# Splitting the second layer's output weights during part 1, and loading values, keys and half of the raw weights in the second half of each batch

## Chip, cores and metric

One of a Trainium2 chip's cores runs the kernel. The metric is device microseconds from start to end of one execution; less is better. Besides the times there is one execution under the hardware profiler, with a trace of every instruction and DMA packet.

## What is computed

Attention through 32 packed queries per head, then two feed-forward blocks on the result, all in fp32:

```python
def sm_attn(qq, kk, vv):                  # scale = 1/sqrt(64)
    a = softmax(scale * qq @ kk.T); return a @ vv
p_packed = sm_attn(p, k, v)               # p: 8 x 8 x 32 x 64;  q, k, v: 8 x 8 x 576 x 64
x = sm_attn(q, p_packed, p_packed)        # then as 4608 tokens x 512
x = maximum(maximum(x @ w1, x @ w2), x @ w3) @ w_out     # 512 -> 768 -> 512
g = softplus(x @ w_in2)                                  # 512 -> 2048
return g @ w_out2                                        # 2048 -> 512
```

The weights arrive as 64-bit numbers and are turned into fp32 in the kernel ("narrowing").

## The kernel before

**Numbers as pairs.** A matmul on TensorE that should keep fp32's precision is done with operands split into a high part `hi` in the format fp32r and the rest `lo`, as three matmuls: hi by hi, hi by lo, lo by hi. A split is two instructions (L125 to L128): ScalarE copies the source into `hi`, then VectorE (or GpSimd) computes `lo = src - hi`.

**Part 1** goes through the eight batches (attention and the first block). In each batch of the loop at L827 (n = 1 to 6) TensorE does the first block of batch n (18 units `U`, 12 matmuls each; four blocks `L`, 36 each) with the attention of batch n + 1 in between. Everything is put into instruction order by hand: the string `batch` (L815) lists names, each appearance advances that step up to its next `yield`, and every engine, SP's queue of DMA issues among them, keeps that order strictly. The names that matter here: `Lq0..3`, `Lk0..3`, `Lv`, `Lp` load raw queries, keys, values and packed queries; `Tq`, `Tk` transpose them; `S` and `A` are the score matmuls, `V` the values, `AX` the second softmax; `LS` splits a maxout result; `D` issues the stores of finished tokens. Beside this the loop prepares the weights of part 2: `R` (L770) issues a load of one 512 KB block of raw 64-bit weights, `N` (L762) narrows the oldest loaded block once `AHEAD` of them have been issued (GpSimd `low_bits`, ScalarE `rebase`, VectorE `combine`), `W` (L697) issues the stores of what is ready, and `Q` (L758) is an empty step. There are 32 blocks: 16 of the input weights `wi2`, then 16 of the output weights `wo2` (L689). Two blocks of `wo2` give, with four subtractions on GpSimd (L748 to L754), the left sides of seven products: both layers of part 2 use Strassen's scheme, so seven products P1 to P7 stand for eight. For the output weights these seven fp32 matrices of 128 x 256 per pair are stored to DRAM as `wof`.

The last batch (L853) has no attention to do and prepares part 2 instead: `loadx`, `sumx`, `splitx` for tokens, `load`, `sum`, `split` for weights.

**Part 2** (from L985) runs the second block in five chunks of tokens, c = 0 to 4: three of 2 x 512 and two of 2 x 384. In a chunk layer 3 has eight steps j (`layer3`, L1050, 42 matmuls each at L1047) and layer 4 has 28 slots v (`layer4`, L1121, 12 matmuls each at L1140), 336 matmuls in each layer. A slot multiplies a split activation tile, `ghi` and `glo` (`split_g`, L1106, three slots ahead, three buffers each), with a weight tile `wc` of seven products. The tiles wc, 1792 KB each, stand in a ring of three. From chunk 1 on they are read back already split, from `wic` (layer 3) and `woc` (layer 4) in DRAM (`get_weights`, L1027). In chunk 0 they are made first: layer 3's from `wi32` by sums and a split, layer 4's by loading seven units of `wof` (`load_units`, L998) and splitting them (`split_weights`, L1012, two halves of 128 x 1024 and 128 x 768), and each is stored by `put_weights` (L1021). For layer 4 this is done at fixed slots (L1229 to L1237):

```python
for t in range(6):
    v = 7 * t // 2 + 1
    for part in range(2):
        jobs[v + part].append((split_weights, FP + t + 2, part))
    if t >= 1 and FP + t + 3 < STEP:
        jobs[v + 1].append((load_weights, FP + t + 3))
    ...
    jobs[v + 2].append((put_weights, FP + t + 2))
```

and for the first two of the eight tiles in steps j = 6, 7 of layer 3 (L1206). Layer 4's VectorE also forms sums and differences of activations (`form`, L1104), sums and splits the next chunk's tokens (`sum_x2`, `split_x2`, at slots 6, 11, 15, 20 and 7, 12, 16, 21 in chunk 0) and moves results out of PSUM (`result`, slots 13, 19, 23, 27).

The functions that the diff touches, and what calls them:

Of the kernel before, what the change touches and what calls it, by code (L numbers as in the profile page):

```python
# [19 lines left out]
def packed_attention_maxout_softplus(  # L20
# [22 lines left out]
    nc = tc.nc  # L43
# [34 lines left out]
    wof = dram.tile([len(PRODUCTS), FP, P, 2 * P], F32, name="wof")  # L78
    woc = dram.tile([FP, P, 2 * 7 * 2 * P], F32, name="woc")
# [58 lines left out]
    nwp = a_ctx.enter_context(tc.tile_pool(name="nwp", bufs=3))  # L138
# [8 lines left out]
    tp = at_ctx.enter_context(tc.tile_pool(name="tp", bufs=2, side="right"))  # L147
    stp = at_ctx.enter_context(tc.tile_pool(name="stp", bufs=5, side="right"))
# [540 lines left out]
    to_narrow = [  # L689
# [4 lines left out]
    ] + [(wo2[f * P : f * P + P, :], (f % FP, f // FP)) for j in range(FP) for f in (j, j + FP)]  # L694
# [6 lines left out]

    def units(j, *names):
        at = [PRODUCTS.index(name) for name in names]
        if len(at) == 1:
            return wof[at[0], j]
        step = at[1] - at[0]
        return wof[at[0] : at[1] + 1 : step, j].rearrange("i p x -> p i x")
# [9 lines left out]
    def narrow_wo_steps(raw64, j, k):  # L717
# [23 lines left out]
        if k == 0:  # L741
            upper[j] = b
            to_store.append((units(j, "P1"), b[:, 0]))
            return
        to_store.append((units(j, "P2", "P3"), b))
# [9 lines left out]
        to_store.append((units(j, "P6", "P5"), t[:, 0:2]))  # L755
        to_store.append((units(j, "P7", "P4"), t[:, 2:4]))

    def split_next():  # L758
        return
        yield  # L760

# [15 lines left out]
    AHEAD = 2  # L777

    def in_batch(n, name):
# [10 lines left out]
        if a == "PW":  # L790
            return packed_weight_steps(n if i else m, i)
        return {
            "Lv": lambda: once(load_v, m),
# [22 lines left out]
            U0 W0 Lq0 D3 N0 PW1 U0 Lq1 N0 U1 PW1 PW1 PP U2 U1 PP W1 N1 Lq2 U3 U2 LS0 LS0 U4  # L816
            U3 N1 W2 R0 N2 PW2 U4 S PW2 Lq3 Lp N2 SX0 U5 Lv SX1 SX0 PW2 W3 SX1 U6 U5 R1 LS1
            VS0 VS1 U7 LS1 U6 Lk0 Tq0 N3 U8 U7 Tq1 Lk1 PW3 U8 LS2 E0 N3 PW3 LS2 E1 R2 U9 E0
            PW3 W4 E1 U10 Lk2 U9 Tq2 N4 U11 U10 Tq3 U12 U11 Lk3 LS3 PW4 R3 N4 LS3 U12 W5 V
            PW4 PW4 U13 VS0 VS1 N5 U14 U13 R4 U15 U14 N5 LS4 LS4 PT U15 U16 PT U17 U16 A U17  # L820
            LS5 PW0 AX0 LS5 AX1 L0 PW0 AX0 R5 AX1 AX0 AX1 AX0 PW0 AX1 AX0 L1 L0 AX1 AX0 AX1
            D0 AX0 AX1 AX0 AX1 X0 L2 L1 X0 X1 X1 D1 Tk0 Tk1 Tk2 L3 L2 Tk3 D2 L3
    """
    with tc.manual_schedule(engines={E.PE, E.DVE, E.Activation, E.Pool, E.SP}):
        for g in range(NH):
            transpose_kq(2, g, "k")
        for n in range(1, B - 1):  # L827
# [170 lines left out]
    def load_units(t):  # L998
        u = wus[FP + t] = up.tile([P, 8, 2, P], F32, tag="u", name="wu")
        flat = wof.rearrange("i j p x -> (i j) p x")  # L1000
        nc.sync.dma_start(
            out=u[:, 1:8].rearrange("p m b x -> p m (b x)"),
            in_=flat[7 * t : 7 * t + 7].rearrange("m p x -> p m x"),
        )

    def load_weights(s):
        if s < FP:
            load_pair(s)
        elif s < STEP:
            load_units(s - FP)  # L1010

# [9 lines left out]
    def put_weights(s):  # L1021
        nc.sync.dma_start(
            out=(wic[s] if s < FP else woc[s - FP]),
            in_=pairs[s].rearrange("p h a k x -> p (h a k x)").bitcast(F32),
        )

    def get_weights(s):  # L1027
        if STEP <= s < STEP * NCH:
            r = s % STEP
            nc.sync.dma_start(  # L1030
                out=pair_tile(s).rearrange("p h a k x -> p (h a k x)").bitcast(F32),
                in_=(wic[r] if r < FP else woc[r - FP]),
            )
# [87 lines left out]
    def layer4(c, v):  # L1121
# [8 lines left out]
        for i in range(2):  # L1130
            u = 2 * (v % NU) + i
            tile_no, at = divmod(pos * FP + u, 7)
            w = pairs[STEP * c + FP + tile_no]
# [180 lines left out]
```

## Time and profile before

| | |
|---|---|
| three runs, us | 1224.98, 1220.55, 1224.32 (median 1224.32) |
| the profiled execution | 1225.36 us, of which the span of its instructions is 1223.6 us |
| mean granted TensorE clock | 0.993 of full speed |
| busy in the span | TensorE matmuls 98%, weight loads 86% (beside them), VectorE 68%, ScalarE 43%, GpSimd 17% |
| moved by DMA | 272.26 MB, on average 223 GB/s |

The page of the profile gives one execution. "Busy" is the time in which an engine's instructions run; idle time is put down to what ended it last. In the trace PE is TensorE's matmul side, PEld its weight loads, DVE VectorE, ACT ScalarE, POOL GpSimd, and SPq the queue of DMA issues on SP. A line such as L128 can be a helper's, so groups are told apart by the names of the tiles: `glo<-a,ghi` and `wc<-wu,wc` are both splits of L128.

### The profile page before, as it was taken

How to read it: one execution, taken by the hardware profiler on the slowest of the kernel's cores; microseconds unless marked ns; L12 is line 12 of the kernel's file. 1: busy time of each engine (PE TensorE's matmuls, PEld its weight loads, DVE VectorE, ACT ScalarE, POOL GpSimd, SP SyncE). 2: the span in 40 equal slices, each digit the busy share in tenths (PEclk: the TensorE clock that was granted, in tenths of full speed). 3: DMA queues.
4: the chain of work that ended last, by engine and by line, in shares of the span. 5: the costliest groups of instructions: out<-in, count | busy, mean ns of one | idle time of the engine just before them, and what ended most of it. 6: DMA issues, size and time to landing. Idle time of an engine off the chain costs nothing.

```text
span 1223.6 us, 21279 instructions
## 1 busy us (share of the span) xinstructions
PE 1196.2 (98%) x8599; PEld 1055.3 (86%) x8599; DVE 829.1 (68%) x1182; ACT 528.4 (43%) x782; POOL 211.0 (17%) x224
## 2 busy tenths in 40 slices
PE   8899999999999999999979999999999999999998
PEld 6688989898989899888757888888888899999998
DVE  2976656575666648678999456894568745874585
ACT  4744443435253434545555234552345423542343
POOL 1422212123242502241000031000310012000100
PEclk9999999999999999999989999999999999999999
DMA  9898686859696721667677955469554597678665
GB/s 244 262 251 196 175 217 179 220 168 255 184 245 190 226 70 36 240 252 269 226 241 282 327 195 191 181 211 331 188 193 181 197 364 267 241 236 320 250 255 144
DMA packets 117283, 272.26 MB, mean 223 GB/s; under 512 B 14784, under 2 KB 90304, under 8 KB 106944
## 3 DMA queue, kind: packets, MB, share of 16 engines
q1 hardware_dynamic: 114976, 269.13, 69.1%
q10 hardware_dynamic: 2208, 1.77, 0.5%
q8 instruction: 67, 1.10, 0.4%
q14 instruction: 32, 0.26, 0.1%
HBM read 211.09 MB, written 59.77 MB: 221 GB/s over the span
## 4 chain that ended last, share of the span: by engine, by line
PE 87%; DVE 7%; DMA 3%; issue 1%; ACT 1%; SPq 0%; DVEq 0%; ACTq 0%
PE ps L482 31%; PE ps L1047 27%; PE ps L1140 22%; PE ps_w L460 3%; DVE glo L128 2%; PE ps_s L287 2%; DVE x2lo L128 1%; DMA wc<-wic 1%; DVE wc L128 1%; DMA qraw<-in_q_dram 1%; PE ps_v L358 1%; PE ps_e L331 1%; DVE a L1104 1%; DMA wu<-wof 1%; DMA praw<-in_p_dram 0%
## 5 line engine op out<-in xcount | busy, mean ns | idle before, releaser
L1047 PE MATMUL ps<-x2hi,wc 128*128 128x512 f32 (+1 forms) x1120 | 322.1, 367 | 2.5 <-DMA wc<-wic 1.1
L1140 PE MATMUL ps<-ghi,wc 128*128 128x512 f32 (+1 forms) x1120 | 323.8, 369 | 0.4 <-ACT ghi L126 0.4
L1061 DVE TENSOR_TENSOR h<-h,ps 128x512 f32<-128x512 f32 (+1 forms) x280 | 173.0, 632 | 156.9 <-PE ps L1047 110.6
L1047 PEld LDWEIGHTS ps<-x2hi,wc 128*128 128x128 f32 x1120 | 207.2, 188 | 29.8 <-DVE h L1061 1.4
L1140 PEld LDWEIGHTS ps<-ghi,wc 128*128 128x128 f32 x1120 | 208.3, 189 | 27.1 <-ACT ghi L126 0.8
L1140 PE MATMUL ps<-glo,wc 128*128 128x512 f32 (+1 forms) x560 | 209.1, 373 | 8.9 <-DVE glo L128 8.5
L1047 PE MATMUL ps<-x2lo,wc 128*128 128x512 f32 (+1 forms) x560 | 205.6, 367 | 0.0
L1082 ACT ACTIVATE a<-h 128x512 f32<-128x512 f32 (+1 forms) x160 | 89.3, 585 | 221.9 <-DVE h L1061 210.2
L126 ACT ACTIVATE ghi<-a 128x1024 fp32r<-128x1024 f32 (+1 forms) x120 | 115.4, 972 | 97.4 <-PE ps L1140 88.2
L128 DVE TENSOR_TENSOR glo<-a,ghi 128x1024 fp32r<-128x1024 f32 (+1 forms) x120 | 131.7, 1110 | 31.7 <-ACT ghi L126 31.5
L1104 POOL TENSOR_TENSOR a<-a,a 128x512 f32<-128x512 f32 (+1 forms) x32 | 36.9, 1155 | 553.3 <-ACT a L1082 553.3
L1140 PEld LDWEIGHTS ps<-glo,wc 128*128 128x128 f32 x560 | 105.8, 189 | 29.8 <-DVE glo L128 16.6
L482 PE MATMUL ps<-a2hi,pwhi 128*128 128x288 f32 x576 | 128.5, 305 | 0.1
L482 PE MATMUL ps<-a2hi,pwlo 128*128 128x288 f32 x576 | 123.2, 295 | 0.4 <-DVE pwlo L128 0.4
L482 PE MATMUL ps<-a2lo,pwhi 128*128 128x288 f32 x576 | 123.2, 296 | 0.0
L1047 PEld LDWEIGHTS ps<-x2lo,wc 128*128 128x128 f32 x560 | 105.1, 188 | 13.2
L511 DVE TENSOR_TENSOR m<-ps,m 128x576 f32<-128x576 f32 x96 | 72.5, 755 | 57.0 <-PE ps L482 55.2
L482 PEld LDWEIGHTS ps<-a2hi,pwhi 128*128 128x128 f32 x576 | 91.6, 189 | 16.8 <-ACT m L509 5.3
L482 PEld LDWEIGHTS ps<-a2hi,pwlo 128*128 128x128 f32 x576 | 92.6, 189 | 0.7 <-DVE pwlo L128 0.7
L482 PEld LDWEIGHTS ps<-a2lo,pwhi 128*128 128x128 f32 x576 | 92.8, 189 | 0.0
L128 POOL TENSOR_TENSOR hlo<-m,hhi 128x576 fp32r<-128x576 f32 x41 | 59.1, 1440 | 189.9 <-ACT hhi L126 165.2
L482 PE MATMUL ps<-hhi,wo_hi 128*128 128x288 f32 x384 | 83.1, 298 | 0.0
(107 smaller groups left out, 1470.1 us busy)
## 6 DMA issues: line engine op xcount, KB each, us to landing
wc<-wic SPq DMA_DIRECT2D x32, 1792.0 KB, 8.8
wc<-woc SPq DMA_DIRECT2D x32, 1792.0 KB, 7.4
qraw<-in_q_dram SPq DMA_DIRECT2D x112, 140.0 KB, 3.8
wic<-wc SPq DMA_DIRECT2D x8, 1792.0 KB
woc<-wc SPq DMA_DIRECT2D x8, 1792.0 KB, 11.3
kraw<-in_k_dram SPq DMA_DIRECT2D x96, 140.0 KB, 5.5
vt<-in_v_dram SPq DMA_DIRECT2D x8, 1152.0 KB, 11.0
wraw<-in_moe_w_dram SPq DMA_DIRECT2D x18, 512.0 KB, 7.5
```

What stands on the lines that cost most here:

```text
L126: nc.scalar.activation(out=hi, in_=src, func=AF.Copy)
L128: engine.tensor_tensor(out=lo, in0=src, in1=hi.bitcast(F32), op=ALU.subtract)
L287: nc.tensor.matmul(ps[G][cols, hh, :HS], w[rows, cols], x[rows, g, hh * HS : hh * HS + HS], start=True, stop=True,)
L331: nc.tensor.transpose(ps[: 32 * TI, i // hi, (i % hi) * P : (i % hi) * P + P], e[:, i], ident,)
L460: nc.tensor.matmul(ps[cols, G, : units * P].rearrange("p (w x) -> p w x", w=units), ppT[n][rows, cols], wsb[rows, 4 * c : 4 * c + units, g ...
L482: nc.tensor.matmul(o, w, xx, start=first, stop=last)
L511: nc.vector.tensor_tensor(out=m, in0=ps[:, :, :HS], in1=ms[n, f], op=ALU.max)
L1047: nc.tensor.matmul(out, l, r, start=(i == 0), stop=(i == len(terms) - 1))
L1061: add(out=h[:, o], in0=h[:, a], in1=ps, op=ALU.add)
L1082: nc.scalar.activation(out=g[half, k][:, j, :wide], in_=h[:, 2 * k + half], func=AF.Softplus)
L1104: engine.tensor_tensor(out=out, in0=in0, in1=in1, op=op)
L1140: nc.tensor.matmul(ps[b][:, :wide], l, r, start=first and u == 0 and head, stop=u == FP - 1 and tail, skip_group_check=not first,)
```

## The change

The seven products of the output weights are split where they are made, in part 1. Each pair of `wo2` blocks now queues four splits; the formerly empty step `Q` does one of them (ScalarE copies to `hi`, VectorE subtracts in place), and the next `W` stores both parts into `woc`, whose layout becomes one 2 KB row (hi, lo) per product, unit and partition. `wof`, its loads, the splits and the `put_weights` of layer 4 in chunk 0 go, and `get_weights` reads `woc` in chunk 0 as in the others, seven rows per partition instead of one of 14 KB. The order of the raw blocks is mixed (two of `wo2`, two of `wi2`, ...), `AHEAD` falls from 2 to 1, the tiles for narrowing get five buffers instead of three and move to the memory that is given up before the last batch. In the batch's order `Lv` loads the values one batch ahead behind `V`, the four `Lk` go behind `Tq3`, and three of the six `R` into the second half.

```diff
-    wof = dram.tile([len(PRODUCTS), FP, P, 2 * P], F32, name="wof")
-    woc = dram.tile([FP, P, 2 * 7 * 2 * P], F32, name="woc")
+    woc = dram.tile([len(PRODUCTS), FP, P, 2, 2 * P], F32, name="woc")
 
...
-    nwp = a_ctx.enter_context(tc.tile_pool(name="nwp", bufs=3))
+    nwp = at_ctx.enter_context(tc.tile_pool(name="nwp", bufs=5, side="right"))
...
-    to_narrow = [
+    wi_narrow = [
         (wi2[e * P : e * P + P, c * 1024 : c * 1024 + 1024],
          wi_blocks(c, e))
         for c in range(DF2 // 512)
         for e in range(KC)
-    ] + [(wo2[f * P : f * P + P, :], (f % FP, f // FP)) for j in range(FP) for f in (j, j + FP)]
+    ]
+    wo_narrow = [
+        (wo2[f * P : f * P + P, :], (f % FP, f // FP)) for j in range(FP) for f in (j, j + FP)
+    ]
+    to_narrow = []
+    for j in range(FP):
+        to_narrow += wo_narrow[2 * j : 2 * j + 2] + wi_narrow[2 * j : 2 * j + 2]
...
             upper[j] = b
-            to_store.append((units(j, "P1"), b[:, 0]))
             return
-        to_store.append((units(j, "P2", "P3"), b))
...
-        to_store.append((units(j, "P6", "P5"), t[:, 0:2]))
-        to_store.append((units(j, "P7", "P4"), t[:, 2:4]))
+        to_split.append((j, ("P1",), a[:, 0:1], a[:, 1:2]))
+        to_split.append((j, ("P6", "P5"), t[:, 0:2], None))
+        to_split.append((j, ("P2", "P3"), b, None))
+        to_split.append((j, ("P7", "P4"), t[:, 2:4], None))
 
     def split_next():
-        return
-        yield
+
+        if not to_split:
+            return
+        j, names, x, hi = to_split.pop(0)
+        at = [PRODUCTS.index(name) for name in names]
+        step = at[1] - at[0] if len(at) > 1 else 1
+        dst = woc[at[0] : at[-1] + 1 : step, j].rearrange("i p h x -> p i h x")
+        if hi is None:
+            hi = nwp.tile([P, 512], F32, tag="x32", name="hi32")
+            hi = hi.rearrange("p (i x) -> p i x", x=2 * P)
+        hi, lo = hi.bitcast(F32R), x.bitcast(F32R)
+        nc.scalar.activation(out=hi, in_=x, func=AF.Copy)
+        yield
+        nc.vector.tensor_tensor(out=lo, in0=x, in1=hi.bitcast(F32), op=ALU.subtract)
+        for h, half in enumerate((hi, lo)):
+            to_store.append((dst[:, :, h], half.bitcast(F32)))
...
-    AHEAD = 2
+    AHEAD = 1
...
-            "Lv": lambda: once(load_v, m),
+            "Lv": lambda: once(load_v, m + 1) if m + 1 < B else none,
...
     batch = """
-            U0 W0 Lq0 D3 N0 PW1 U0 Lq1 N0 U1 PW1 PW1 PP U2 U1 PP W1 N1 Lq2 U3 U2 LS0 LS0 U4
-            U3 N1 W2 R0 N2 PW2 U4 S PW2 Lq3 Lp N2 SX0 U5 Lv SX1 SX0 PW2 W3 SX1 U6 U5 R1 LS1
-            VS0 VS1 U7 LS1 U6 Lk0 Tq0 N3 U8 U7 Tq1 Lk1 PW3 U8 LS2 E0 N3 PW3 LS2 E1 R2 U9 E0
-            PW3 W4 E1 U10 Lk2 U9 Tq2 N4 U11 U10 Tq3 U12 U11 Lk3 LS3 PW4 R3 N4 LS3 U12 W5 V
-            PW4 PW4 U13 VS0 VS1 N5 U14 U13 R4 U15 U14 N5 LS4 LS4 PT U15 U16 PT U17 U16 A U17
-            LS5 PW0 AX0 LS5 AX1 L0 PW0 AX0 R5 AX1 AX0 AX1 AX0 PW0 AX1 AX0 L1 L0 AX1 AX0 AX1
-            D0 AX0 AX1 AX0 AX1 X0 L2 L1 X0 X1 X1 D1 Tk0 Tk1 Tk2 L3 L2 Tk3 D2 L3
+            U0 W6 Lp Lq0 Q0 N0 Q0 PW1 U0 N0 Lq1 U1 PW1 D3 PW1 R0 W0 PP U2 U1 PP Q1 N1 U3 U2
+            LS0 Lq2 Q1 LS0 U4 U3 N1 Q2 N2 PW2 U4 W1 Q2 S PW2 R1 N2 SX0 U5 Lq3 SX1 SX0 PW2 W2
+            SX1 U6 U5 LS1 VS0 VS1 U7 LS1 U6 Tq0 Q3 N3 U8 U7 Q4 Tq1 R2 PW3 U8 Q3 LS2 E0 N3
+            PW3 LS2 E1 Q4 U9 E0 PW3 E1 W3 U10 U9 Tq2 Q5 N4 U11 U10 Tq3 Q6 U12 U11 Lk0 LS3 Q5
+            PW4 N4 LS3 Q6 U12 V PW4 PW4 Q7 U13 VS0 W4 VS1 N5 Q8 U14 U13 Lk1 Q7 U15 U14 Lv N5
+            LS4 Q8 LS4 PT U15 U16 R3 PT W5 U17 U16 Lk2 A U17 LS5 PW0 AX0 R4 LS5 AX1 L0 PW0
+            AX0 AX1 AX0 Lk3 AX1 AX0 PW0 AX1 AX0 L1 L0 AX1 R5 AX0 AX1 AX0 AX1 D0 AX0 AX1 X0
+            L2 L1 X0 X1 X1 Tk0 Tk1 D1 Tk2 L3 L2 Tk3 D2 L3
     """
     with tc.manual_schedule(engines={E.PE, E.DVE, E.Activation, E.Pool, E.SP}):
         for g in range(NH):
             transpose_kq(2, g, "k")
+        load_v(2)
         for n in range(1, B - 1):
...
-    def load_units(t):
...
-    def load_weights(s):
...
     def put_weights(s):
         nc.sync.dma_start(
-            out=(wic[s] if s < FP else woc[s - FP]),
+            out=wic[s],
             in_=pairs[s].rearrange("p h a k x -> p (h a k x)").bitcast(F32),
         )
 
     def get_weights(s):
-        if STEP <= s < STEP * NCH:
-            r = s % STEP
-            nc.sync.dma_start(
-                out=pair_tile(s).rearrange("p h a k x -> p (h a k x)").bitcast(F32),
-                in_=(wic[r] if r < FP else woc[r - FP]),
-            )
+        r = s % STEP
+        if s >= STEP * NCH or s < FP:
+            return
+        flat = pair_tile(s).rearrange("p h a k x -> p (h a k x)").bitcast(F32)
+        if r < FP:
+            nc.sync.dma_start(out=flat, in_=wic[r])
+            return
+        rows = woc.rearrange("i j p h x -> (i j) p (h x)")[7 * (r - FP) : 7 * (r - FP) + 7]
+        nc.sync.dma_start(
+            out=flat.rearrange("p (m x) -> p m x", m=7), in_=rows.rearrange("m p x -> p m x")
+        )
...
-            w = pairs[STEP * c + FP + tile_no]
+            w = pairs[STEP * c + FP + tile_no].rearrange("p h a k x -> p (h a k x)")
+            w = w.rearrange("p (a h k x) -> p h a k x", a=7, h=2, k=2)
...
-                    for part in range(2):
-                        aside[1 + part].append((split_weights, j + 2, part))
-                    aside[3] += [(load_weights, j + 4), (put_weights, j + 2)]
+                        for part in range(2):
+                            aside[1 + part].append((split_weights, j + 2, part))
+                        if j + 4 < FP:
+                            aside[3].append((load_pair, j + 4))
+                        aside[3].append((put_weights, j + 2))
...
-                for t in range(6):
-                    v = 7 * t // 2 + 1
-                    for part in range(2):
-                        jobs[v + part].append((split_weights, FP + t + 2, part))
-                    if t >= 1 and FP + t + 3 < STEP:
-                        jobs[v + 1].append((load_weights, FP + t + 3))
-                    if t == 0:
-                        jobs[v + 1].append((load_x2, c + 1, 0))
-                    jobs[v + 2].append((put_weights, FP + t + 2))
+                jobs[2].append((load_x2, c + 1, 0))
```

## Rows read from the trace of the kernel before

**Rows 1.** Windows: length, PE, PEld, DVE, ACT, POOL busy (instructions), clock, DMA share, GB/s

```profile
337.00:395.70 58.70, 58.70 (x617) 53.07 (x616) 39.27 (x75) 24.05 (x39) 21.18 (x24) 1.00 0.79 222
...
507.70:584.00 76.30, 76.28 (x336) 63.17 (x337) 56.72 (x74) 37.95 (x56) 23.48 (x24) 1.00 0.73 265
584.00:676.20 92.20, 83.14 (x338) 63.88 (x337) 81.98 (x92) 48.60 (x55) 0.00 (x0) 0.96 0.70 242
676.20:752.60 76.40, 76.35 (x338) 62.86 (x336) 38.34 (x57) 24.09 (x39) 14.71 (x15) 1.00 0.71 250
752.60:829.00 76.40, 76.40 (x337) 62.95 (x336) 66.03 (x70) 38.74 (x43) 1.30 (x1) 1.00 0.56 191
...
981.80:1040.10 58.30, 58.30 (x338) 58.15 (x336) 30.74 (x57) 19.75 (x39) 12.76 (x15) 1.00 0.87 318
```

**Rows 2.** Waits of PE, whole span: us in total, times, longest us

```profile
PE ps L1140 <- DVE glo L128: 8.5, 8, 3.6
```

**Rows 3.** PE in order of time, chunk 0's layer 4: start, us, what, [idle before]

```profile
630.10 0.39 PE L1140 MATMUL ps<-glo,wc 128*128 128x512 f32 x1
...
635.16 0.80 PE L1140 MATMUL ps<-glo,wc 128*128 128x512 f32 x1 [3.55 <-DVE glo L128]
...
636.61 0.63 PE L1140 MATMUL ps<-glo,wc 128*128 128x512 f32 x1
```

**Rows 4.** Windows for tile wc alone, chunk 0's layer 4: columns without POOL

```profile
584.00:676.20 92.20, 83.14 (x338) 63.88 (x337) 13.00 (x12) 11.31 (x12) 0.96 0.70 242
```

**Rows 5.** Groups of DVE and ACT, chunk 0's layer 4: busy us, mean ns | idle

```profile
L885 DVE TENSOR_TENSOR xu<-xu 128x256 f32<-128x256 f32 x16 | 6.1, 420 | 0.1
...
L128 DVE TENSOR_TENSOR x2lo<-xu,x2hi 128x1024 fp32r<-128x1024 f32 x4 | 4.9, 1218 | 0.0
L1186 DVE STREAM_TRANSPOSE o<-mid 128x512 f32<-128x512 f32 x6 | 4.3, 712 | 0.2
L1184 DVE TENSOR_TENSOR mid<-mid,ps 128x512 f32<-128x512 f32 x6 | 4.0, 664 | 0.0
L128 DVE TENSOR_TENSOR x2lo<-xu,x2hi 128x768 fp32r<-128x768 f32 x4 | 3.8, 952 | 0.0
...
L126 ACT ACTIVATE ghi<-a 128x1024 fp32r<-128x1024 f32 x22 | 22.7, 1051 | 11.9 <-PE ps L1140 11.9
L126 ACT ACTIVATE wc<-wu 128x1024 fp32r<-128x1024 f32 x6 | 6.3, 1056 | 11.0 <-DMA wu<-wof 6.6 <-DMA xu<-x2d 4.4
```

**Rows 6.** Chain of waits, chunk 0's layer 4: start, us, what

```profile
602.87 1.14 DVE glo L128
```

**Rows 7.** Groups of DVE and ACT in the batch of rows 1, columns as there

```profile
L128 DVE TENSOR_TENSOR pwlo<-ps_w,pwhi 128x512 fp32r<-128x512 f32 x1 | 0.7, 691 | 0.6 <-ACT pwhi L126 0.6
...
L722 ACT ACTIVATE x<-raw 128x512 f32<-128x512 f32 x6 | 4.0, 674 | 9.2 <-DMA raw<-in_moe_w_out_dram 4.7 <-DMA kraw<-in_k_dram 4.5
```

**Rows 8.** Waits of all engines, batches 2 to 6 of the loop

```profile
ACT x L86 <- DMA raw<-in_moe_w_in_dram: 13.8, 4, 4.7
```

**Rows 9.** SP's queue, ACT and the chain on PE near the loop's start

```profile
98.41 5.14 SPq L553 DMA_DIRECT2D x2d<-xs  x2
...
110.16 0.65 ACT L509 ACTIVATE m<-ps 128x576 f32<-128x576 f32 x1
...
112.74 0.97 PE ps_s L287 x32
```

**Rows 10.** Tile raw: ns min/median/max of an operation, and its DMAs

```profile
L732 DVE SCALAR_TENSOR_TENSOR x<-x,raw x64: 276/284/1535, 285.2 to 422.3; 128x128 int32<-128x128 int32 x64
...
DMA to landing us min/median/max: 2.6/6.8/10.9
```

**Rows 11.** The page's DMA issues: KB each, median us to landing

```profile
wc<-woc SPq DMA_DIRECT2D x32, 1792.0 KB, 7.4
...
wu<-wof SPq DMA_DIRECT2D x8, 896.0 KB, 8.6
wof<-raw SPq DMA_DIRECT2D x16, 256.0 KB, 2.6
```

More of the change, by code (lines that the diff above doesn't have):

```diff
@@ L700, in store_narrowed @@
             nc.sync.dma_start(out=dst, in_=x)
[L702 to L707, printed above, removed]
     def narrow_wi_steps(raw64, dst):
@@ L996, in packed_attention_maxout_softplus @@
     STEP = 2 * FP
-    def load_units(t):
-        u = wus[FP + t] = up.tile([P, 8, 2, P], F32, tag="u", name="wu")
-        flat = wof.rearrange("i j p x -> (i j) p x")
-        nc.sync.dma_start(
-            out=u[:, 1:8].rearrange("p m b x -> p m (b x)"),
-            in_=flat[7 * t : 7 * t + 7].rearrange("m p x -> p m x"),
-        )
-    def load_weights(s):
[L1007 to L1010, printed above, removed]
     def split_weights(s, part):
@@ L1027, in get_weights @@
     def get_weights(s):
-        if STEP <= s < STEP * NCH:
-            r = s % STEP
-            nc.sync.dma_start(
-                out=pair_tile(s).rearrange("p h a k x -> p (h a k x)").bitcast(F32),
-                in_=(wic[r] if r < FP else woc[r - FP]),
-            )
+        r = s % STEP
[9 more added lines that the diff above has]
+        )
     def bank(name):
```

## Prediction, made before the changed kernel ran

> **What bounds the kernel now.** TensorE does, almost everywhere, so the first question is where it is not full. The windows cut at the stages answer it [rows 1]: a batch of part 1, chunk 0's two layers, chunk 1's two, and a layer of the narrower chunk 3. In a batch of part 1 PE is busy for the whole 58.70 us; the six batches of the loop all look so. In part 2 chunks 0 to 2 have the same 336 matmuls in every layer, and chunk 1 shows what they cost when nothing is late: 76.40 us in layer 3 and 76.40 in layer 4. Chunk 0's layer 3 takes the same, but its layer 4 takes 92.20 us, with PE busy for 83.14, VectorE for 81.98 and a granted clock of 0.96. That is 15.8 us over. The list of PE's waits names the cause [rows 2]: 8.5 us in 8 waits for `glo`, the low part of an activation split, the longest 3.6 us. In order of time that one stands at 635.16 [rows 3], after 3.55 us of idling, and behind it a matmul takes 0.63 us that took 0.39 before: with the granted clock at 0.96 over the stretch, TensorE ran for a few microseconds at 1.2 instead of 2.4 GHz. So the 15.8 are the recorded waits, the half clock behind the longest, and small gaps that the modelled ends cover.
>
> Why is `glo` late? In chunk 0 VectorE also splits weights: 12 instructions on `wc`, 13.00 us, with 11.31 us on ScalarE [rows 4], and ScalarE's copies of them sit idle for 11.0 us, 6.6 of it for the load of `wof` [rows 5]. Both engines work strictly in order, so a weight split whose data is not there holds the activation splits behind it. Chunk 1's VectorE does the same work without weights in 66.03 us and nobody waits [rows 1].
>
> **Removed from chunk 0.** Of layer 4: the 12 VectorE and 12 ScalarE instructions, four of the eight loads of `wof` and their waits, and six stores of `woc`. VectorE keeps 81.98 - 13.00 = 69.0 us in 76.4, three more than chunk 1, because 16 instead of 8 of the sums on `xu` stand here (6.1 us, so 3.0 for eight) [rows 5]. Since 69 of 76 is tight, I walk the worst stretch, slots 6 to 13. A slot is 76.4 / 28 = 2.73 us, eight are 21.8. VectorE has in them eight `glo` and six forms of the same size at 1.14 each from start to start [rows 6], two groups of four sums (4 x 0.42, overlapping, 1.5), two splits of tokens (1.22 + 0.95, overlapping, 2.0) and one result (2 x (0.71 + 0.66), 2.7) [rows 5]: 16.0 + 3.0 + 4.0 + 2.7 = 25.7. It falls 3.9 us behind. `glo` is made up to two slots ahead, 5.5 us, of which its own copy and subtraction take 1.05 + 1.14 [rows 5, 6], leaving 3.3. So it is about 0.6 us late around slot 14, and then recovers, since slots 14, 17 and 18 hold one `glo` alone. Layer 4 comes out at 77.0: a gain of 15.2 us. Its bounds are 15.8 (no wait left) and 8 (half of the waits stay, because the burst is worse than my walk).
>
> Layer 3 of chunk 0 loses four such VectorE splits too. I put that at nothing: PE is busy for 76.28 of its 76.30 us [rows 1].
>
> **Weights read back in chunk 0.** Eight loads of `woc` come in, 1792 KB each, median 7.4 us to landing [rows 11], as in the other chunks. A tile is asked for when the one three before it is released, and two tiles last 2 x 76.4 / 8 = 19 us, so it costs nothing while a load lands within that. What is new in all five chunks is that a row of 14 KB becomes seven of 2 KB. The trace has no such load. From below it is the 7.4 us; from above it is `wof`, in pieces of 1 KB: 896 KB in 8.6 us [rows 11], so 17.2 us for a whole tile. I take about 8, since the pieces are nearer in effect to the `x2d` and 14 KB traffic that shares these engines than to a load issued just before a 1792 KB store, as `wof`'s are. Cost 0; the upper end is a rival below.
>
> **Added to part 1.** 32 splits, about 5.3 in a batch: 24 of 128 x 512, 8 of half that. The nearest rows are 0.69 us on VectorE and 0.67 on ScalarE [rows 7], so at most 3.7 and 3.6 us in a batch. VectorE then has 43 of 58.7 us and ScalarE 28 [rows 1]; the Q steps lie in the first three fifths of the batch, one or two in ten microseconds, so VectorE may be full for a moment, with PSUM's four buffers as cover. Stores rise from 32 to 64, hi and lo apart, and SP's queue gets some 0.4 us of issuing for each: 2 us in a batch. GpSimd does no more than before, only spread. All of it lies beside TensorE, which has no idle time in these batches to hide it twice: if it delays the emptying of PSUM, it costs. How much cover there is the trace shows: ScalarE stands up to 4.7 us before a narrowing copy whose load is late [rows 8], and PE does not notice. I went through the order for longer holds, counting time by the 360 long matmuls of a batch (58.7 us): blocks are narrowed 12 to 25 us behind their load once the loop runs, and a `hi` buffer is reused at the earliest one or two steps behind the store that frees it, where a store of 256 KB lands in 2.6 us [rows 11]. That is within 4.7 us. Cost 0, bounds 0 and 2 us a batch.
>
> **The one place without a lead** is the loop's first batch. With nothing in flight, N1 pops the block that R0 has issued two steps before. R0 now stands behind D3, whose stores hold SP until 98.41 + 5.14 = 103.6 [rows 9]. The load lands 6.8 us later in the median and 10.9 at most [rows 10]: 110.4 to 114.5. Behind N1 on ScalarE wait an `hhi` and the `m` copy, which ran at 110.16 [rows 9]; 0.67 + 0.68 + 0.65 later than the landing the PSUM buffer is free, at 112.4 to 116.5. The scores that need it begin at 112.74 [rows 9]. So 0 to 3.8 us, and since the values' 1152 KB now go ahead of it, 1.5.
>
> **Moved transfers.** `Lk` and `Lv` lie later. The last, `Lk3`, still has the blocks L1 to L3 before its transpose, 108 of the batch's 360 long matmuls, so over a quarter of its time; the values have most of a batch. DMA's share is 0.79 over a batch [rows 1]; nobody waits for it on PE today, so spreading it gains nothing by itself.
>
> **Sum.** 1225.36 (the profiled execution, span 1223.6 and 1.8 around it) - 15.2 + 1.5 = 1211.7. That execution was 1.0 above the median of the three, 1224.32; on the median it makes **1210.5 us**.
>
> **Rivals.**
> - *Forecast, 0.74:* as summed, 1205 to 1214.
> - *VectorE still limits chunk 0, 0.10:* the burst of slots 6 to 16 leaves half of the waits: 1218 at worst. For it: 69 of 76.4 us. Against it: chunk 1 with 66 has no wait.
> - *Part 1 pays, 0.09:* steps in the fixed order wait in ScalarE's queue for GpSimd or for a slot's store, with the copies that empty PSUM behind them; at 2 us in each of five batches 1220 to 1222, no change. For it: a VectorE instruction of 0.28 us with two inputs in SBUF took up to 1.54 [rows 10], so something does hold it, and each of the 32 subtractions could meet 1.25 us of that, 7 us of VectorE in a batch. Against it: 43 + 7 are still below 58.7. The Trainium skill ("SBUF — State Buffer", section "SBUF: two separate sides") speaks against the change here: GpSimd and a VectorE instruction with two SBUF inputs exclude each other for the whole instruction. The long instruction just named agrees with that; by this rule the split moves from a stage where GpSimd is idle to one where it is busy.
> - *The 2 KB rows, 0.07:* slower. If a tile takes the 17.2 us worked out from `wof`, it is covered in chunks 0 to 2 (19 us), but in the two chunks of 384 columns two tiles last only 2 x 58.3 / 8 = 14.6 us [rows 1], so each of 16 tiles is 2.6 us late: +42, less 15, about 1251. It decides above 14.6 us. Against it: the long row and the 1 KB row differ by a factor of 2.3 that a store beside them explains at least in part.
>
> That the splits would still be done in chunk 0 is excluded: the diff takes their instructions out.
>
> **Range and chances.** A measurement of this kernel tells about 0.5% (6 us) from no change. Forecast and first rival hold 0.84 of the chance; the low end is the full 15.8 with nothing paid at the loop's start (1208.5) and 3.5 us for the scatter of the three runs; the high end the first rival: 1205 to 1218. Faster 0.84, same 0.09, slower 0.07.
>
> **What would show it.** Right: chunk 0's layer 4 in 76.4 to 78 us at clock 1.0 and VectorE busy for about 69; no `wc` on VectorE or ScalarE there; batches still 58.7 us each; the first perhaps 60. `woc` landing in 7 to 9 us. Wrong: PE waits in the batches for `m` or `ps`, or `PE <- DMA wc<-woc`, or a layer 4 above 80 us.

## The result, and the profile after

The changed kernel takes **1213.24 us** in the median of five runs (1212.02 to 1214.98), the kernel before 1224.98 beside it (1220.55 to 1227.72): a ratio of 0.9906, 95% interval [0.988, 0.9933]. A second measurement, the first experiment below, gave 0.9902 [0.9878, 0.9926]. The forecast was 1210.5, in a range of 1205 to 1218.

The windows of the changed kernel, with the columns of [rows 1]: the loop's first stretch from the scores `S` of one batch to those of the next, the third, and chunk 0's layer 4.

```profile
111.68:172.44 60.76, 59.16 (x629) 53.15 (x628) 41.65 (x71) 27.13 (x45) 16.98 (x17) 1.00 0.78 205
...
231.10:290.00 58.90, 58.87 (x625) 53.00 (x617) 43.68 (x74) 27.49 (x45) 16.32 (x16) 1.00 0.86 241
585.90:663.20 77.30, 76.84 (x338) 63.00 (x337) 69.07 (x79) 39.09 (x43) 0.00 (x0) 1.00 0.65 206
```

Layer 4 is down from 92.20 us [rows 1] to 77.30, at a full clock, and VectorE from 81.98 to 69.07. Of PE's waits there one is left, where there were 8.5 us in 8 [rows 2]:

```profile
PE ps L1146 <- DVE glo L127: 0.5, 1, 0.5
```

The page's row on the tiles that are read back, which answers to [rows 11]; chunk 0's eight are now among them:

```profile
wc<-woc SPq DMA_DIRECT2D x40, 1792.0 KB, 8.0
```

The account by stretches, measured from one start to the next in both traces: the span falls by 13.4 us, from 1223.6 to 1210.2. Chunk 0's layer 4 gives 14.8. The loop's first stretch takes 2.1 back, the third and the fifth 0.28 each. The nine other layers of part 2 give 0.4 in sum, the opening before the loop's first scores 0.9; none of the steps accounts for these two.

**The first stretch.** In order of time on SP's queue, ScalarE and TensorE of the changed kernel:

```profile
94.77 9.25 SPq L186 DMA_DIRECT2D qraw<-in_q_dram  x8
...
105.38 0.35 SPq L786 DMA_DIRECT2D raw<-in_moe_w_out_dram  x1
```

```profile
111.42 0.68 ACT L720 ACTIVATE x<-raw 128x512 f32<-128x512 f32 x1 [5.06 <-DMA raw<-in_moe_w_out_dram]
```

```profile
113.25 1.20 PE L286 MATMUL ps_s<-vT,pT 64*32 64x288 f32 x30 [0.97 <-ACT m L508]
115.08 0.54 PE L481 MATMUL ps<-a2hi,pwhi 128*128 128x288 f32 x2 [0.62 <-DVE m L510]
```

The load of the first raw block is issued at 105.38, behind eight loads of queries that hold SP for 9.25 us and behind D3. It lands at 111.4; the narrowing copy, which waits for it, holds ScalarE until then, the copy of `m` behind it comes late, and PE waits 0.97 and 0.62 us.

**The third stretch.** VectorE, GpSimd and the weight loads in order of time:

```profile
240.36 2.12 DVE L730 SCALAR_TENSOR_TENSOR x<-x,raw 128x128 int32<-128x128 int32 x4
242.41 1.13 DVE L770 TENSOR_TENSOR raw<-raw,hi 128x512 fp32r<-128x512 f32 x1
243.46 1.21 DVE L127 TENSOR_TENSOR pwlo<-ps_w,pwhi 128x1024 fp32r<-128x1024 f32 x1
```

```profile
240.65 1.49 POOL L127 TENSOR_TENSOR hlo<-m,hhi 128x576 fp32r<-128x576 f32 x1 [2.10 <-ACT hhi L125]
242.22 0.80 POOL L95 TENSOR_SCALAR raw<-raw 128x512 int32<-128x512 uint8 x1
```

```profile
244.72 0.30 PEld L481 LDWEIGHTS ps<-a2hi,pwhi 128*128 128x128 f32 x2 [0.27 <-DVE pwlo L127]
```

Four combining steps that take 0.89 us elsewhere take 2.12 beside GpSimd's `hlo`, the new split 1.13 instead of 0.68 beside its next instruction: 1.7 us more. `pwlo`, the low part of the packed weights, stands behind them on VectorE and comes late; the weight load waits 0.27 us for it, and PE, which has no room in these stretches, loses 0.28 us. The fifth stretch has the same wait, the second and the fourth have none.

### The profile page after: what moved, and what is told of

Read it like the earlier page. It is cut to its first block, busy times and chain, and to the rows that moved or that the text cites. A ratio compares the mean times of both kernels' runs of the same rounds, so it can differ in the third digit from the quotient of the medians.

```text
span 1210.2 us, 21326 instructions
## 1 busy us (share of the span) xinstructions
PE 1188.7 (98%) x8599; PEld 1053.2 (87%) x8599; DVE 839.2 (69%) x1198; ACT 531.5 (44%) x798; POOL 214.9 (18%) x224
## 4 chain that ended last, share of the span: by engine, by line
PE 87%; DVE 5%; DMA 5%; issue 1%; ACT 1%; POOL 0%; SPq 0%; DVEq 0%; ACTq 0%; POOLq 0%
PE ps L481 28%; PE ps L1052 28%; PE ps L1146 26%; PE ps_w L459 2%; DMA qraw<-in_q_dram 2%; PE ps_s L286 1%; DVE glo L127 1%; DVE x2lo L127 1%; DMA wc<-wic 1%; PE ps_v L357 1%; DMA woraw<-in_moe_w_out_dram 1%; PE ps_e L330 1%; DMA raw<-in_moe_w_out_dram 0%; DMA wraw<-in_moe_w_dram 0%; DVE a L1109 0%
## 5 line engine op out<-in xcount | busy, mean ns | idle before, releaser
L1146 PE MATMUL ps<-glo,wc 128*128 128x512 f32 (+1 forms) x560 | 206.6, 369 | 0.7 <-DVE glo L127 0.6
```

The costliest lines, as they stand in the source:

```text
L1146: nc.tensor.matmul(ps[b][:, :wide], l, r, start=first and u == 0 and head, stop=u == FP - 1 and tail, skip_group_check=not first,)
```

## Experiments

Stretches 1 to 5 run from the scores of one batch of the loop to those of the next, in the profiled run; L4 is chunk 0's layer 4. The opening ahead of stretch 1 is the same program in e2, e7 and e8 and took 117.3, 112.2 and 115.2 us there, so what an edit does to the loop is read from the stretches.

| kernel | median us (range) | ratio to before, 95% | stretches 1 to 5 | L4 |
|---|---|---|---|---|
| before | 1224.98 (1220.55 to 1227.72) | 1 | 58.65 58.65 58.66 58.65 58.65 | 92.05 |
| changed | 1213.24 (1212.02 to 1214.98) | 0.9906 [0.988, 0.9933] | 60.76 58.66 58.93 58.65 58.93 | 77.27 |
| again_after | 1214.72 (1209.55 to 1216.78) | 0.9902 [0.9878, 0.9926] | 62.45 58.66 58.91 58.66 58.93 | 77.23 |
| e1_lead | 1220.57 (1216.24 to 1225.79) | 0.9952 [0.9932, 0.9972] | 63.65 58.75 62.25 58.75 60.73 | 77.23 |
| e2_no_shift | 1226.75 (1222.25 to 1237.64) | 1.0025 [1.0, 1.005] | 58.73 60.60 63.03 63.03 62.98 | 77.21 |
| e3_dve_back | 1222.9, one run | beside 1223.66 | 63.23 58.66 58.94 58.66 58.93 | 85.91 |
| e4_low_on_gpsimd | 1231.93, one run | beside 1223.66 | 58.65, the last 59.59 | 96.91 |
| e5_spread_only | 1226.12 (1225.13 to 1230.29) | 1.0013 [0.9998, 1.0027] | 60.88 58.65 58.65 58.65 58.66 | 92.02 |
| e6_keys_back | 1212.37 (1210.52 to 1214.91) | 0.9894 [0.987, 0.9919] | 60.80 58.64 58.87 58.66 58.87 | 77.21 |
| e7_values_back | 1217.85 (1216.42 to 1219.28) | 0.9941 [0.9921, 0.996] | 58.66 58.64 61.39 58.64 63.48 | 77.19 |
| e8_stores_first | 1218.73 (1215.97 to 1223.68) | 0.9947 [0.9922, 0.9972] | 58.65 58.66 63.75 59.59 63.07 | 77.23 |
| e9_r0_early | 1209.65 (1207.25 to 1210.97) | 0.9869 [0.9845, 0.9892] | 58.66 58.64 58.92 58.64 58.91 | 77.19 |
| e10_four_buffers | 1218.45 (1215.16 to 1220.98) | 0.9939 [0.9917, 0.9961] | 60.71 58.64 60.91 60.05 60.42 | 77.20 |
| e11_seven_buffers | 1213.71 (1211.37 to 1216.1) | 0.9909 [0.9884, 0.9934] | 58.65 58.64 58.87 58.65 59.13 | 77.17 |

**The changed kernel again (again_after)**, with no edit, as the measure of the others.

> The changed kernel once more, as the base for the other runs of this call. Theory: chunk 0's layer 4 in 77 to 78 us at clock 1.0, the loop's first batch 2 us longer than the others, the ratio to the kernel before 0.988 to 0.993.

Measured 1214.72. The gain is the same; the first stretch varies, 62.45 here.

**A lead for the raw blocks (e1_lead).**

```diff
+        for _ in range(3):
+            load_next()
         load_v(2)
```

> Three raw blocks are loaded ahead of the loop, so that the first batch narrows with the same lead as the others. Theory (the 2.1 us of the first batch are ScalarE standing before the copy of a block loaded two steps earlier): the waits of the scores for m and of the next unit for m in the first batch go, and the kernel gets 1.5 to 2.5 us faster than the changed one. Rival (the first batch is longer because values and queries of 1.7 MB stand in the DMA queues there, whoever waits for them): 1.5 MB more go ahead of it, the wait moves to another tile, and the time stays within 0.5 us or gets up to 3 us worse.

It became 6 us slower than the changed kernel. PE's waits from the opening to the loop's end:

```profile
PE ps L481 <- ACT e L312: 6.2, 3, 2.1
PE ps_v L357 <- DMA vt<-in_v_dram: 3.6, 1, 3.6
```

Three blocks ahead of the loop hold up the opening's other loads, the values among them (that wait is 0.9 us in the changed kernel), and later stretches gain waits for `e`. The lead also moves every narrowing by one step, which may be what these waits come from; no run shows it. Loading more, earlier, is not the mend for the first stretch.

**The splits without the moved transfers (e2_no_shift).** Values, packed queries and keys go back to where they are issued in the kernel before. The moved names, in the order of the batch:

```diff
-            U0 W6 Lp Lq0
+            U0 W6 Lq0
...
-            U5 Lq3 SX1
+            U5 Lv Lq3 Lp SX1
...
-            U6 Tq0 Q3 N3 U8 U7 Q4 Tq1 R2
+            U6 Lk0 Tq0 Q3 N3 U8 U7 Q4 Tq1 Lk1 R2
...
-            W3 U10 U9
+            W3 U10 Lk2 U9
...
-            U12 U11 Lk0 LS3
+            U12 U11 Lk3 LS3
...
-            U13 Lk1 Q7 U15 U14 Lv N5
+            U13 Q7 U15 U14 N5
...
-            U16 Lk2 A
+            U16 A
...
-            AX0 Lk3 AX1
+            AX0 AX1
...
-            "Lv": lambda: once(load_v, m + 1) if m + 1 < B else none,
+            "Lv": lambda: once(load_v, m),
...
-        load_v(2)
```

> The splits stay in part 1, but values, keys and packed queries are loaded at the places where the kernel before loads them, in the first half of the batch; raw blocks as in the changed kernel. Theory (all of the gain is chunk 0's layer 4, the moved transfers give nothing by themselves and the DMA has slack of several us everywhere): within 1.5 us of the changed kernel, perhaps without the first batch's 2 us, since the values are no longer ahead of the first block. Rival (the moved transfers are what makes room for the splits: DMA share 1.0 in the first half): raw blocks land later, ScalarE stands before them by more than the 4.7 us that PE has been seen not to notice, batches of 59 to 61 us, 3 to 12 us slower than the changed kernel.

The whole gain is gone: 1.0025 [1.0, 1.005], with layer 4 still at 77.21 us. In the loop the loss lies in stretches 2 to 5, 1.9 to 4.4 us each. SP, ScalarE and PE in the fourth:

```profile
304.20 10.02 SPq L186 DMA_DIRECT2D kraw<-in_k_dram  x8
...
315.31 0.97 SPq L705 DMA_DIRECT2D woc<-x  x2
```

```profile
320.19 0.66 ACT L85 ACTIVATE x<-raw 128x512 f32<-128x512 f32 x1 [7.19 <-DMA woc<-x]
```

```profile
322.98 0.62 PE L481 MATMUL ps<-a2hi,pwhi 128*128 128x288 f32 x2 [2.60 <-ACT m L508]
323.40 0.69 PE L481 MATMUL ps<-a2lo,pwhi 128*128 128x288 f32 x2
```

Two stores of split parts stand in SP's queue behind eight loads of keys, which hold it for 10.02 us. The narrowing buffers come free late, ScalarE stands 7.19 us before a copy that needs one, the copies that empty PSUM stand behind it, and PE waits 2.60 us; then its matmul pairs take 0.69 us where they took 0.42. For some 3 us it ran at 1.2 GHz: the granted clock from 320 to 330 us is 0.83. This is the rival of part 1 in the prediction, at up to twice its price. Of the two expectations above neither named it: the first saw no loss, and the rival had ScalarE waiting for raw blocks, not for stores.

**VectorE's time put back (e3_dve_back).** In chunk 0's layer 4, at the slots where the splits were, twelve VectorE instructions of the same size that leave their tile as it is:

```diff
+                def again(part):
+                    y = g[1, 1][:, 0:2, : (512, 384)[part]]
+                    nc.vector.tensor_tensor(out=y, in0=y, in1=y, op=ALU.max)
+
+                for t in range(6):
+                    for part in range(2):
+                        jobs[7 * t // 2 + 1 + part].append((again, part))
```

> The changed kernel with 12 VectorE instructions given back to chunk 0's layer 4, at the slots and in the sizes of the former weight splits (128 x 1024 and 128 x 768, two SBUF inputs, the maximum of a tile with itself, so no value changes), but without ScalarE's copies and without loads of raw units. Theory A (VectorE's time alone made the waits): 69 + 12 = 81 us of VectorE do not fit 76.4, so layer 4 gets at least 82 and, with the waits' bunching and the half clock, 86 to 92 us. Theory B (what held the stage was ScalarE standing in order before copies whose load was late): only what exceeds the stage is paid, layer 4 in 79 to 84 us, at clock 1.0.

The stage's window, columns as above, and PE's waits in it:

```profile
582.00:668.00 86.00, 79.92 (x338) 62.13 (x337) 81.40 (x92) 41.19 (x46) 0.00 (x0) 1.00 0.59 193
```

```profile
PE ps L1146 <- DVE glo L127: 5.8, 7, 1.4
```

Layer 4 takes 85.91 us: VectorE's time alone makes 8.6 of the 14.8 us. Theory A had 82 us or more; the full clock is theory B's. The waits are nearly as many as before but none is over 1.4 us, and the granted clock is 1.00. The other 6.1 us are left by subtraction. What e3 does not give back is ScalarE's copies behind late loads of `wof` [rows 5] and the loads and stores themselves; the longest wait and the half clock behind it [rows 3] went with them. No run takes these apart.

**The kernel before, with the low parts on GpSimd (e4_low_on_gpsimd).** GpSimd is idle in that stage [rows 1].

```diff
-    def split_weights(s, part):
+    def split_weights(s, part, engine=nc.vector):
...
-        split(u[:, a + 1 : b + 1], t[:, 0, a:b], t[:, 1, a:b])
+        split(u[:, a + 1 : b + 1], t[:, 0, a:b], t[:, 1, a:b], engine)
...
-                        jobs[v + part].append((split_weights, FP + t + 2, part))
+                        jobs[v + part].append((split_weights, FP + t + 2, part, nc.gpsimd))
```

> The kernel before, in which the low parts of the weight splits of chunk 0's layer 4 are made by GpSimd, which is idle there, instead of VectorE; ScalarE's copies and the loads stay. Theory A (VectorE's time): VectorE at 69 us as in the changed kernel, layer 4 in 77 to 81 us. Theory B (ScalarE before the loads): the 11 us of ScalarE's idling before these copies stay, layer 4 in 83 to 90 us. Theory C (GpSimd and VectorE exclude each other on two SBUF inputs): about 12 x 2.3 us of GpSimd hold VectorE's splits, single VectorE splits of up to 3.5 us, layer 4 at 92 us or more.

Slower: layer 4 takes 96.91 us. VectorE and GpSimd in order of time:

```profile
598.70 2.83 DVE L128 TENSOR_TENSOR glo<-a,ghi 128x1024 fp32r<-128x1024 f32 x1
...
602.60 1.21 DVE L128 TENSOR_TENSOR glo<-a,ghi 128x1024 fp32r<-128x1024 f32 x1
...
608.27 3.42 DVE L1104 TENSOR_TENSOR a<-a,mid 128x1024 f32<-128x1024 f32 x1
```

```profile
597.92 2.53 POOL L128 TENSOR_TENSOR wc<-wu,wc 128x768 fp32r<-128x768 f32 x1 [0.22 <-ACT wc L126]
607.60 5.80 POOL L128 TENSOR_TENSOR wc<-wu,wc 128x1024 fp32r<-128x1024 f32 x2 [7.15 <-ACT wc L126]
```

```profile
580.80:677.70 96.90, 84.17 (x338) 64.86 (x337) 93.06 (x83) 52.70 (x60) 32.21 (x12) 0.95 0.68 247
```

Here a VectorE instruction that meets one of GpSimd takes 2.83 or 3.42 us where it takes 1.21, as theory C had it. What is handed to GpSimd is paid again in VectorE's time, 93.06 us in the stage's window against 81.98 before [rows 1], so GpSimd did not hide the splits in this stage.

**The moved transfers without the splits (e5_spread_only).** The kernel before with the changed order, without its `Q`:

```diff
-    AHEAD = 2
+    AHEAD = 1
...
-            "Lv": lambda: once(load_v, m),
+            "Lv": lambda: once(load_v, m + 1) if m + 1 < B else none,
...
+        load_v(2)
         for n in range(1, B - 1):
```

> The kernel before with the changed kernel's order of transfers (values one batch ahead, keys and half of the raw blocks in the second half, narrowing one block behind) and without the moved splits. Theory: layer 4 of chunk 0 stays at 91 to 93 us, batches at 58.7, the first batch up to 2 us longer: 0 to 3 us slower than the kernel before. Rival (the spread brings part of the gain): 3 us or more faster than the kernel before, with shorter batches or a shorter chunk 0.

No gain: 1.0013 [0.9998, 1.0027], and the first stretch, at 60.88 us, pays 2.2 us, about as in the changed kernel. By themselves the moved transfers are worth nothing; with the splits they are worth 12.0 to 13.5 us (1226.75 in e2 against 1214.72 and 1213.24; by the sums of the five stretches 10.8 and 12.4). Which of them is it?

**Keys back (e6_keys_back)** and **values back (e7_values_back)**, each alone, in the changed kernel: of e2's edit the `Lk` tokens, or the `Lp` and `Lv` tokens with the two lines on `load_v`.

```diff
-            U6 Tq0 Q3 N3 U8 U7 Q4 Tq1 R2
+            U6 Lk0 Tq0 Q3 N3 U8 U7 Q4 Tq1 Lk1 R2
...
-            W3 U10 U9
+            W3 U10 Lk2 U9
...
-            U12 U11 Lk0 LS3
+            U12 U11 Lk3 LS3
```

```diff
-            U0 W6 Lp Lq0
+            U0 W6 Lq0
...
-            U5 Lq3 SX1
+            U5 Lv Lq3 Lp SX1
...
-            U15 U14 Lv N5
+            U15 U14 N5
```

> The changed kernel with only the four loads of keys (Lk) back at their old places; the values stay a batch ahead. Theory D (order of SP's queue: the two groups of keys' loads, which hold SP for 10 us until buffers come free, stand ahead of the stores that free ScalarE's hi buffers): the keys alone bring back most of the loss, batches 2 to 6 of the loop at 61 to 63 us, total 1222 to 1227, and ScalarE shows waits of several us for a store of woc. Rival E (the batch's first half holds too many bytes, and values and keys count by their bytes: 1152 KB and 1152 KB): about half of the loss comes back, batches of some 60.5 us, total 1217 to 1221.

> The changed kernel with only the loads of the values and of the packed queries (Lv, Lp) back at their old places; the keys stay late. Theory D: the loads of the values are few and do not hold SP, so the batches stay at 58.7 to 59.3 us, total 1211 to 1216, and the first batch of the loop may even be shorter. Rival E: half of the loss comes back, batches of some 60.5 us, total 1217 to 1221.

I had it the wrong way round. Keys back costs nothing (1212.37). Values back costs 3 to 5 us (1217.85): 7.0 in stretches 3 and 5, less the 2.1 that the first no longer takes. Both together cost 12.0 to 13.5. Neither theory fits: not the bytes alone, since the page counts 16 loads of keys of 140 KB in a batch, 2240 KB and not the 1152 of my expectation, more than the values; and not the hold on SP alone. With the values back, in the fifth stretch, SP:

```profile
348.93 0.39 SPq L198 DMA_DIRECT2D vt<-in_v_dram  x1
349.37 2.16 SPq L186 DMA_DIRECT2D qraw<-in_q_dram  x4
351.58 1.22 SPq L207 DMA_DIRECT2D praw<-in_p_dram  x2
352.89 0.66 SPq L705 DMA_DIRECT2D woc<-hi  x1
```

and ScalarE and PE:

```profile
347.67 0.62 ACT L768 ACTIVATE hi<-raw 128x512 fp32r<-128x512 f32 x1
...
361.73 0.63 ACT L768 ACTIVATE hi<-raw 128x512 fp32r<-128x512 f32 x1 [5.40 <-DMA woc<-hi]
```

```profile
364.59 0.53 PE L481 MATMUL ps<-a2hi,pwhi 128*128 128x288 f32 x2 [3.04 <-ACT e1T L337]
...
366.11 0.68 PE L481 MATMUL ps<-a2lo,pwhi 128*128 128x288 f32 x2
```

The `hi` made at 347.67 waits for its store until 352.89, behind values, queries and packed queries, and the 1152 KB of values, issued at 348.93, are then ahead of it in the DMA engines too. By the trace the next split's copy waits 5.40 us for a store of `woc<-hi`; the last one issued before that wait began is this one. With the keys back there is one such wait in each of two stretches, 2.00 us and, in the fourth, the one shown here, and nobody waits behind either:

```profile
306.19 0.67 ACT L85 ACTIVATE x<-raw 128x512 f32<-128x512 f32 x1 [3.05 <-DMA wi<-x]
```

So a hold of ScalarE of 3.05 us costs TensorE nothing in that place, and one of 5.40 in the other costs it 3.04, with matmul pairs of 0.68 us behind it.

**Stores ahead of the second group of keys (e8_stores_first).** e2 with one name moved:

```diff
-            Tq1 Lk1 R2 PW3 U8 Q3 LS2 E0 N3 PW3 LS2 E1 Q4 U9 E0 PW3 E1 W3 U10 Lk2
+            Tq1 R2 PW3 U8 Q3 LS2 E0 N3 PW3 LS2 E1 Q4 U9 E0 PW3 E1 W3 Lk1 U10 Lk2
```

> The second experiment (splits kept, values and keys at their old places) with one token moved: the second group of keys (Lk1) is issued behind the stores W3 instead of some ten steps ahead of them. The bytes of the batch's first half stay nearly the same, SP's order differs. Theory D: the stores no longer stand behind the keys, ScalarE's wait of 7 us for a store of woc goes, batches 2 to 6 at 58.7 to 60 us, total 1213 to 1219. Rival E: no help, batches still 62 to 63 us and total 1223 to 1228.

1218.73: by the medians 8.0 us of e2's loss are gone by the order on SP alone, with the same bytes in the batch. The traces show less: the five stretches are 4.7 us shorter in sum than in e2, the second by 1.9, the fourth by 3.4, the third 0.7 longer; the rest of the difference between the two profiled runs lies in the opening and in part 2, which the edit leaves as they are. So the order matters, and it is not all. Theory D was right in the total and wrong in that all would be well: stretches 3 and 5 stay at 63 us, much as in e7. What is left there are waits for stores again (the loop's stretches):

```profile
ACT hi L768 <- DMA woc<-hi: 10.8, 2, 5.7
...
PE ps L481 <- ACT e1T L337: 6.0, 2, 3.4
```

In the second stretch, at 58.66 us, nobody waits behind one of 3.90:

```profile
191.02 0.69 ACT L85 ACTIVATE x<-raw 128x512 f32<-128x512 f32 x1 [3.90 <-DMA woc<-hi]
```

**The first raw block's load moved (e9_r0_early).**

```diff
+            order = batch.split()
+            if n == 1:
+                order.remove("R0")
+                order.insert(order.index("Lq1"), "R0")
-            for name in batch.split():
+            for name in order:
```

> The changed kernel, in the first batch of the loop only, with the first raw block's load (R0) issued ahead of Lq1 and D3 instead of behind them. My account of the first batch (the narrowing copy waits for a load that SP could issue only behind D3): the load is issued some 9 us earlier, the copy does not wait, the first batch takes 58.7 to 59.2 us instead of 60.8, and the total is 1.5 to 2 us below the changed kernel's, about 1211. Rival: the queries behind it or the copies of the opening set the first batch's end, and it stays above 60 us.

SP, ScalarE, and the window of the first stretch:

```profile
97.47 0.37 SPq L786 DMA_DIRECT2D raw<-in_moe_w_out_dram  x1
```

```profile
108.90 0.66 ACT L720 ACTIVATE x<-raw 128x512 f32<-128x512 f32 x1 [2.49 <-DMA raw<-in_moe_w_out_dram]
```

```profile
111.70:170.40 58.70, 58.70 (x630) 53.09 (x621) 40.08 (x68) 25.83 (x42) 15.16 (x16) 1.00 0.82 217
```

Issued 7.9 us earlier, the load still makes ScalarE wait 2.49 us, which costs PE nothing; the first stretch is down to 58.66 us. At 1209.65 us this is the fastest version of the study, 0.9869 [0.9845, 0.9892], 3.6 us below the changed kernel's median. The two intervals overlap; what the trace shows of the gain is the 2.1 us of this stretch.

**Four narrowing buffers (e10_four_buffers)** in the changed kernel, and **seven (e11_seven_buffers)** in the one with the values back.

```diff
-    nwp = at_ctx.enter_context(tc.tile_pool(name="nwp", bufs=5, side="right"))
+    nwp = at_ctx.enter_context(tc.tile_pool(name="nwp", bufs=4, side="right"))
```

```diff
-    nwp = at_ctx.enter_context(tc.tile_pool(name="nwp", bufs=5, side="right"))
-    stp = at_ctx.enter_context(tc.tile_pool(name="stp", bufs=5, side="right"))
+    nwp = at_ctx.enter_context(tc.tile_pool(name="nwp", bufs=7, side="right"))
+    stp = at_ctx.enter_context(tc.tile_pool(name="stp", bufs=4, side="right"))
```

> The changed kernel with four buffers for narrowing instead of five, the transfers left where the change puts them. Theory F (what the splits need is a narrowing buffer whose store has landed; moving the values only lets the store land in time): with one buffer fewer ScalarE must wait for stores of woc here too, 3 us or more in several batches, PE waits behind it, and the total is 1216 to 1235. Rival G (TensorE's waits with the values at their old place came from the crowded DMA engines themselves, by another way than the buffers): the transfers are spread here, so a buffer fewer changes nothing, 1211 to 1215.

> The kernel with the values and the packed queries back at their old places, with seven buffers for narrowing instead of five (and four for raw blocks instead of five, which gives the room). The values' load stands ahead of the stores as before. Theory F: ScalarE's two waits of 4.8 and 5.4 us for a store of woc go, and with them PE's waits for e1T; batches 58.7 to 59 us, total 1209 to 1214. Rival G: the batches behind which PE waited stay at 61 to 63 us, total 1215 to 1220. If the fourth raw buffer is what is then missing, POOL waits longer for raw blocks, and the time tells nothing.

Theory F holds in both. With four, ScalarE and PE wait from 100 to 430 us as follows:

```profile
ACT x L85 <- DMA woc<-x: 5.8, 2, 3.1
ACT x L720 <- DMA woc<-hi: 5.2, 2, 3.1
...
PE ps L481 <- ACT e L312: 4.5, 4, 2.0
```

The longest of these, on ScalarE and then on PE:

```profile
235.50 0.67 ACT L85 ACTIVATE x<-raw 128x512 f32<-128x512 f32 x1 [3.10 <-DMA woc<-x]
```

```profile
238.54 0.53 PE L481 MATMUL ps<-a2hi,pwhi 128*128 128x288 f32 x2 [1.98 <-ACT e L312]
```

With seven, the values' load stands where it stood in e7 and ScalarE waits for no store; all that is left of PE's waits in the loop is

```profile
PE ps L481 <- ACT e L312: 0.3, 1, 0.3
```

and 1217.85 becomes 1213.71. So the resource is the narrowing buffer: to let its store go in time, or to have two more of them, comes to the same here, by the stretches (58.87 and 59.13 us where e7 has 61.39 and 63.48).

## Why the prediction was right, and where its steps were not

- **Chunk 0's layer 4: 77.0 us, gain 15.2.** Measured 77.27 and 14.8. The walk through the slots had VectorE at 69.0 us (69.07) and one `glo` some 0.6 us late around slot 14; the one wait left is 0.5 us, near slot 17. That VectorE was the larger cause is shown by e3, 8.6 us; that ScalarE's late loads and the half clock had the rest is argued, by subtraction.
- **Weights read back in chunk 0: 0.** The tiles land in 8.0 us in the median, "about 8"; the first of chunk 0 takes 11.6, more than the 7 to 9 that I had, and PE waits for none. The rival of the 2 KB rows, 17.2 us, is out.
- **Splits in part 1: 0, between 0 and 2 us a batch.** In the change as it is, 0.28 us in each of two stretches. The reason given failed. I set a store's 2.6 us, the median of the stores of `wof`, against 4.7 us by which ScalarE had once stood unnoticed [rows 8], and called that covered. Neither number carries over. A store that is ready can first stand in SP's queue, in e2 behind 10.02 us of keys, and in the changed kernel the stores of `hi` land in up to 5.7 us. What a hold of ScalarE costs depends on its place in the batch: 3.90 us cost nothing in e8, 5.40 cost 3.04 in e7, and 3.10 went with a wait of 1.98 in e10. The splits are free because the transfers moved: without that they cost all of the gain (e2, 1.9 to 4.4 us a stretch, over my upper bound of 2).
- **Moved transfers: "spreading it gains nothing by itself".** True as said (e5) and wrong as a term of this sum: 12.0 to 13.5 us hang on it. I looked for who waits for a transfer in the kernel before, and not for what the new stores would stand behind in SP's queue.
- **The first batch: 1.5, between 0 and 3.8.** Measured 2.1 (3.8 in the second measurement), by the mechanism given: the load landed at 111.4, within the 110.4 to 114.5 forecast, though eight loads of queries held SP longer than D3 did, and e9 removes it. In e7, where the values' 1152 KB do not go ahead of it, it does not arise.
- **The rival of part 1**, at 0.09, named ScalarE's queue and the store rightly, not what makes the store late, and is what e2 and e10 look like. Its second half, GpSimd beside VectorE, is real and cheap here: the new split takes 0.68 to 1.92 us, as the view of tile `hi` in the changed kernel shows (min, median, max in ns), where the form on `x` keeps to 0.68:

```profile
L770 DVE TENSOR_TENSOR raw<-raw,hi x16: 681/1132/1922, 130.6 to 424.7; 128x512 fp32r<-128x512 f32 x16
...
L770 DVE TENSOR_TENSOR x<-x,hi x8: 681/682/693, 135.2 to 423.5; 128x512 fp32r<-128x512 f32 x8
...
DMA to landing us min/median/max: 2.5/2.6/5.7
```

The Trainium skill ("SBUF — State Buffer", section "SBUF: two separate sides") has the two engines exclude each other for a whole instruction when VectorE has two inputs in SBUF and GpSimd reads there too; the trace agrees, here and in e4. In the third stretch `hlo` takes 1.49 us and the four steps beside it 1.23 more than alone; together with the splits' own time that made `pwlo` late and cost the 0.28 us in each of two stretches.

So two terms were right as numbers and not by their reasons. Each half of the change was priced at nothing on its own; the splits alone take back all of the gain (e2), the moved transfers alone gain nothing (e5), and the sum held because the change makes both. That part of the forecast was luck.

On the profiled execution the sum gave 1211.7 us and the run was 1212.02: the misses, 0.4 in layer 4, 0.6 in the first batch and 0.6 in the splits, are met by 1.3 us less in the opening and in part 2, which no step claimed.

## What to carry to other kernels

Before work is moved into a stage that is "not full", follow its stores: what stands ahead of them in the issuing queue, which buffer they free, and which engine blocks in order on that buffer. A change that gains nothing alone, like a transfer issued later, can be the one that makes another free, so test both halves separately and price the pair. Where memory allows, more buffers can buy the same as the reordering; here it was two.

## What was not expected of the hardware

- A queue that issues in order turns a load's wait into a store's delay: eight loads of keys held SP for 10.02 us with stores ready behind them (e2). Moving one group of four behind the stores gave 8.0 us of 1226.75 back in the medians, 4.7 of them in the loop's stretches (e8).
- The same cost is far from additive: keys at their old place 0, values 3 to 5, both 12.0 to 13.5 us. Nor is there one length of a hold of ScalarE that is free: 3.05 and 3.90 us cost nothing in their places with five buffers (e6, e8), and with four, 3.10 us in another place went with a wait of PE of 1.98 (e10).
- GpSimd as helper made its stage slower: twelve subtractions given to it stretched VectorE's instructions of 1.21 us to 2.83 and 3.42, and layer 4 from 92.05 to 96.91 us.
